# Sorting k and v of two batches in natural layout, on 32x32 tiles of the array

## The chip, the cores and the metric

One core of a Trainium2 chip runs the whole kernel. The metric is device time in microseconds (us) of one execution; lower is better. In this document PE is the matrix engine, ACT and DVE are the scalar and vector engines, POOL is the general-purpose engine (here it issues the loads that cast from 32-bit to bfloat16), and SP is the engine that issues the other transfers. SBUF is the on-chip memory of 128 partitions, PSUM the accumulators that PE writes.

## The reference

Sinkhorn attention feeds a squared-ReLU feed-forward network (FFN). There are 4 batches, 8 heads, 768 tokens, 64 features a head, and 8 blocks of 96 tokens.

```python
P = sort_net                                   # [4, 8, 8, 8]
for _ in range(5):                             # Sinkhorn
    P = exp(P - max(P, -1)); P /= sum(P, -1) + 1e-9; P /= sum(P, -2) + 1e-9
k_sorted = einsum('bhij,bhjcd->bhicd', P, k_blocks)   # blocks of k mixed by P
v_sorted = einsum('bhij,bhjcd->bhicd', P, v_blocks)
attn = softmax(q_block @ k_sorted_block.T / 8)        # within each block
x = (attn @ v_sorted_block), heads side by side       # [3072, 512]
out = relu(x @ w_in) ** 2 @ w_out                     # 512 -> 2048 -> 512
```

## The kernel before

**The FFN** works in eight units of 384 tokens (`ffn_unit`, L662). A unit has 16 upward groups (`up`, L671, matmuls at L675: four of 384 moving columns), each followed by a ReLU on ACT (L683) and a square on DVE (L686), and then 12 downward groups (`down`, L699, matmuls at L703: four of 512 columns; four groups make one output tile of 128 tokens, which is copied out of PSUM at L183 or L185 and stored by SP at L719, over three output buffers). These 28 groups a unit are the planner's clock: its "chunks". A unit reads x transposed (`xT`) for half of one batch.

**Attention** works on pairs of heads, four pairs a batch (class `Unit`, L373). For a pair of batches 2 and 3 the steps are these.

- `s_q` (L386, PE L399): twelve PE transposes of q in two column halves of the array, one for each head, and a copy out of PSUM into `qT`.
- `s_sort` for k (L428, PE L443): twelve matmuls, again in two column halves. The stationary is a 64-feature slice of k as loaded, the moving operand is `w_all`, a 128x128 matrix for each head that holds P spread over the token rows (`build_w`, L358, a product of a mask and P on DVE at L361). The result is k sorted and transposed in one step; a copy brings it into `ksT` with the tokens of a block side by side.
- `s_vn` (L530, PE L542): v is sorted with `w_all` as stationary, one matmul of 384 columns a head, and stays in token rows. To bring the rows of a block onto 96 partitions, SP writes it to DRAM (`v_way`, L563) and reads it back (L568).
- `s_sc` (L467, PE L481): two groups of eight score matmuls (64 feature rows, 96 columns), in two row halves of the array; then the exponential on ACT (L497).
- `s_av` (L580, PE L596): two groups of eight matmuls with the sorted v, and the division by the sums on DVE (L606, L607).
- `s_xt` (L626): the result is turned into `xT` by a transposing transfer on SP (L629).

Batches 0 and 1 sort v in the way of k and turn it back with PE transposes (`s_vt`, L505, PE L513).

**The order of the work** is written by a planner while the program is built (class `Plan`, L50). Each operation is entered with an engine, a cost and what it depends on. PE takes from two queues, attention and FFN, each in its own order; an attention group goes first once its due chunk has come and it is ready, and FFN groups go past an attention group that is not ready. A change of the array's mode is planned at 0.1 us (`SWITCH`). "SP" entries are the issue of a transfer and "WAY" entries its flight. `Ring` objects stand for buffers: among them two PSUM slots for sorts, scores and PV (`r2`). Due chunks are given in `lay` (L798): batch 2 between chunks 84 and 112, batch 3 between 140 and 168, while the FFN units for batches 2 and 3 begin at chunks 112 and 168. So batch 2's attention runs beside the fourth FFN unit and batch 3's beside the sixth; the third and the fifth have none beside them. The loads on POOL are not bound to this order and go out when their buffers are free.

**The start.** Until the first FFN group, the Sinkhorn steps run on ACT and DVE, the loads arrive, and the first half of batch 0's attention runs (list `FIRST`, L19). PE is kept at work by fillers, matmuls on a tile of ones (`fill`, L316): 40 at the beginning (`warm`, L322), and, where the plan has a gap over 0.15 us, one of 128 columns for each 0.08 us of it (L852, L853). A mask for `build_w` is folded out of an identity on POOL (`make_mask`, L268).

Of the kernel before, what the change touches and what calls it, by code (L numbers as in the profile page):

```python
# [8 lines left out]
FP32 = mybir.dt.float32  # L9
# [40 lines left out]
class Plan:  # L50
# [4 lines left out]
    TAIL = {"PE": 0.0, "ACT": 0.09, "DVE": 0.06, "POOL": 0.0, "DMA": 0.0, "SP": 0.0, "WAY": 0.0}  # L55
# [65 lines left out]
def kernel(  # L121
# [47 lines left out]
    rqT, rao, rks, ret = Ring(6), Ring(3), Ring(3), Ring(4)  # L169
    AD = ("ACT", "DVE")  # L170
# [20 lines left out]
    v_r = v.rearrange("b h (p a) d -> b p h (a d)", a=NA)  # L191
    w_in_r = moe_w_in.rearrange("(kc p) f -> p kc f", p=128)
# [29 lines left out]
    v_way = nc.dram_tensor("v_way", (B, 2, 128, NA, HP * 66), BF16, kind="Internal").ap()  # L222
# [9 lines left out]
    w_all = const.tile([128, NH, NB, C0], BF16)  # L232
# [33 lines left out]
    mask = const.tile([128, C0], BF16)  # L266

    def make_mask(e):  # L268

        src, w = ident, 64  # L270
        while w >= C0:
            dst = mask if w == C0 else const.tile([128, w], BF16, name=f"fold{w}")
# [3 lines left out]
    for g in range(HP):  # L276
        load(0, 1, 2 * g, 2)
        load(0, 2, 2 * g, 2)
        if g == 0:
            plan.add("POOL", 1.0, make_mask, [id_op])  # L280
# [35 lines left out]
    def fill(n, w):  # L316
        for _ in range(n):
            nc.tensor.matmul(  # L318
                out=p2[0][:, 1, 512 - w:512], lhsT=ones[:, 0:128], rhs=ones[:, 0:w],
                start=True, stop=True)  # L320

    def warm(e):  # L322
        fill(40, 128)
# [47 lines left out]


    class Unit:  # L373


        def __init__(self, b, hp, halves):
            self.b, self.hp, self.halves = b, hp, halves
            self.n, self.old = rks.take()
# [7 lines left out]
    def s_q(b, hp, p0, p1, due=0, after=None, eng=AD):  # L386
# [4 lines left out]
        def mm(e):  # L391
# [11 lines left out]
            if p0 == 0:  # L403
                tiles["qT", b, hp] = att.tile(
                    [128, NB, NA, C0], BF16, tag="qT", name="qT", bufs=6)

        def ev(e):
            copy(e, tiles["qT", b, hp][:, p0 // C0:p1 // C0, :, :],
# [58 lines left out]
    def s_sc(u, due=0):  # L467
# [3 lines left out]
        for hf in u.halves:  # L471
# [4 lines left out]
            def mm(e, hf=hf, st=st, slot=slot):  # L476
                qT = tiles["qT", u.b, u.hp]
                st["p"] = scp = p2[slot]
                for n in range(NQ):
                    for h in range(2):  # L480
                        nc.tensor.matmul(  # L481
                            out=scp[:, h, BLK * n:BLK * (n + 1)],
                            lhsT=u.ksT[64 * h:64 * (h + 1), hf, BLK * n:BLK * n + 128],
                            rhs=qT[64 * h:64 * (h + 1), NQ * hf + n, :, :]
                            .rearrange("p a c -> p (a c)"),
# [7 lines left out]
            rks.use(u.n, pe)  # L493
# [36 lines left out]
    def s_vn(b, g, due):  # L530

        m, oldm = rvn.take()
        evs = []
        for hp in (2 * g, 2 * g + 1):
            st = {}

            slot, old = r2.take()

            def mm(e, hp=hp, st=st, slot=slot):
                st["p"] = p2[slot]  # L540
                for h in range(2):
                    nc.tensor.matmul(  # L542
                        out=st["p"][:, h, 0:NA * D],
                        lhsT=w_all[:, H * b + 2 * hp + h, :, :].rearrange("p i c -> p (i c)"),
                        rhs=qkv[b][2][:, 2 * hp + h, :],
                        start=True, stop=True)

            def ev(e, hp=hp, st=st):
                h0 = 2 * (hp % 2)
                copy(e, vn_r[m][:, :, h0:h0 + 2, 0:D],  # L550
                     st["p"][:, :, 0:NA * D].rearrange("p e (a d) -> p a e d", d=D))

            s2 = slot
            h0 = H * b + 2 * hp
            pe = plan.add("PE", 0.34, mm, [landed[b, 2, HP * g, 0], built[h0], built[h0 + 1]]
                          + old, due)
            readers[b].append(pe)
            op = plan.add(AD, cost_f(2 * NA * D), ev, [pe] + oldm)
            r2.use(s2, pe, op)
# [326 lines left out]
```

## Time and profile before

| what | us |
|---|---|
| time, median of three runs (lowest to highest) | 235.98 (235.05 to 236.11) |
| the profiled execution: its time | 235.18 |
| its span | 232.8 |
| PE, busy in the span | 225.2 |
| ACT, busy | 125.6 |
| DVE, busy | 107.8 |
| POOL, busy | 27.7 |

The span is the time between the first and the last instruction of the profiled execution. Busy times of different engines overlap. The profile names a group of instructions by its line, its engine, its operation and its operands; a count follows, then the sum of busy time, the mean of one in nanoseconds, and the idle time of the engine before them with what ended it. "PEld" is the loading of stationary operands, which overlaps matmuls. Matmuls are pipelined, so the mean of one is longer than the pace of many. The chain of waits is followed back from the last instruction, and gives each piece's start, its length and what it was.

### The profile page before, as it was taken

The numbers are of one execution on the slowest core, as the hardware profiler recorded it, in microseconds if no ns is written. First come the engines' busy times: TensorE is split into PE (matmuls) and PEld (weight loads), VectorE is DVE, ScalarE is ACT, GpSimd is POOL, SyncE is SP. The second block draws the span as 40 slices with busy tenths as digits, with TensorE's granted clock in tenths as the row PEclk, the third lists the DMA queues.
The fourth block names the chain that finished last, engine by engine and source line by source line (L and its number), as shares of the span: only waits on it lengthen the run. The fifth ranks groups of instructions, "written<-read, shape, count | busy, mean of one in ns | idle before, by whom it ended". The sixth has DMA issues, their size and how long they took to land.

```text
span 232.8 us, 5519 instructions
## 1 busy us (share of the span) xinstructions
PE 225.2 (97%) x2283; PEld 133.3 (57%) x2296; DVE 107.8 (46%) x298; ACT 125.6 (54%) x263; POOL 27.7 (12%) x44
## 2 busy tenths in 40 slices
PE   8997999999999999999999999999999999999994
PEld 8876665556666556445655555445665455446553
DVE  5676677317775515205686425105674225105400
ACT  4665676228884347319865247219776257227521
POOL 8963222400005200000000000000000000000000
PEclk9999999999999999999999999999999999999999
DMA  5999999999914995025511340025612530011012
GB/s 78 202 205 206 206 207 204 203 228 236 156 34 59 176 239 106 3 92 189 139 34 37 83 120 3 0 90 189 139 37 49 85 106 1 31 62 45 0 48 92
DMA packets 33145, 25.70 MB, mean 110 GB/s; under 512 B 9952, under 2 KB 29664, under 8 KB 33120
## 3 DMA queue, kind: packets, MB, share of 16 engines
q0 software_dynamic: 16960, 13.63, 37.8%
q1 hardware_dynamic: 16160, 11.71, 18.3%
q8 instruction: 18, 0.29, 0.5%
q14 instruction: 7, 0.06, 0.1%
HBM read 28.89 MB, written 7.91 MB: 158 GB/s over the span
## 4 chain that ended last, share of the span: by engine, by line
PE 87%; DVE 4%; DMA 3%; ACT 3%; issue 1%; ACTq 0%; DVEq 0%
PE op L703 34%; PE hp L675 32%; PE p L318 4%; PE p L481 3%; PE p L596 3%; PE qtp L399 3%; PE p L443 3%; DMA vblk<-v_way 2%; PE op L737 2%; PE vbp L513 1%; DVE ao L607 1%; ACT h L683 1%; DVE h L686 1%; DMA v_way<-vn 1%; PE xtp L644 1%
## 5 line engine op out<-in xcount | busy, mean ns | idle before, releaser
L675 PE MATMUL hp<-xT,w_in_bf 128*128 128x384 bf16 x512 | 92.3, 326 | 0.0
L703 PE MATMUL op<-w_out_bf,h 128*128 128x512 bf16 x355 | 82.4, 379 | 0.8 <-issue 0.2
L683 ACT ACTIVATE h<-hp 128x384 bf16<-128x384 f32 x128 | 62.7, 494 | 22.0 <-PE hp L675 20.8
L686 DVE TENSOR_TENSOR h<-h 128x384 bf16<-128x384 bf16 x128 | 44.2, 355 | 51.7 <-ACT h L683 51.5
L675 PEld LDWEIGHTS <-w_in_bf 128*128 128x128 bf16 x512 | 46.6, 98 | 29.7
L703 PEld LDWEIGHTS <-h 128*128 128x128 bf16 x368 | 34.7, 98 | 39.0
L183 ACT COPY ob<-op 128x512 f32<-128x512 f32 (+1 forms) x24 | 13.6, 568 | 60.2 <-PE op L703 57.6
L497 ACT ACTIVATE et<-p 96x384 bf16<-96x384 f32 x64 | 26.6, 488 | 9.3 <-PE p L481 9.3
L607 DVE TENSOR_TENSOR ao<-p,rec 96x512 bf16<-96x512 f32 x32 | 22.0, 687 | 1.3 <-DVE rec L606 0.2
L318 PE MATMUL p<-ones 128*128 128x128 bf16 x119 | 11.6, 260 | 1.5 <-DVE ones L200 1.1
L185 DVE CAST vn<-p 128x768 bf16<-128x768 f32 x4 | 3.8, 958 | 19.6 <-PE p L542 19.6
L596 PEld LDWEIGHTS <-et 96*128 96x128 bf16 x256 | 10.8, 97 | 3.4 <-issue 0.5
L183 ACT CAST ksT<-p 128x768 bf16<-128x768 f32 (+1 forms) x13 | 9.5, 730 | 3.4 <-PE p L443 3.3
L606 DVE RECIPROCAL rec<-p 96x8 f32<-96x8 f32 x32 | 6.4, 199 | 10.6 <-PE p L596 9.5
L481 PEld LDWEIGHTS <-ksT 64*128 64x128 bf16 x256 | 6.4, 94 | 7.6 <-issue 4.4
L318 PEld LDWEIGHTS <-ones 128*128 128x128 bf16 x119 | 9.4, 121 | 2.0 <-DVE ones L200 1.1
L481 PE MATMUL p<-qT,ksT 64*128 64x96 bf16 x256 | 10.1, 204 | 0.3 <-DVE ao L607 0.2
L239 POOL DMA_DIRECT2D qb<-in_q_dram x8 | 6.0, 751 | 34.8 <-PE qtp L399 26.4
L185 DVE COPY qT<-qtp 128x768 bf16<-128x768 bf16 x8 | 4.5, 556 | 10.1 <-PE qtp L399 10.1
L399 PEld LDWEIGHTS <-qb 128*64 128x64 bf16 (+1 forms) x240 | 6.4, 109 | 4.7 <-issue 4.0
L185 DVE COPY vs<-vbp 96x512 bf16<-96x512 bf16 (+1 forms) x12 | 6.1, 508 | 6.3 <-PE vbp L513 6.2
L399 PE MATMUL qtp<-ident,qb 128*64 128x128 bf16 (+1 forms) x240 | 8.9, 212 | 0.0
(65 smaller groups left out, 131.8 us busy)
## 6 DMA issues: line engine op xcount, KB each, us to landing
out_dram<-ob SPq DMA_DIRECT2D x23, 256.0 KB, 2.0
qb<-in_q_dram POOLq DMA_DIRECT2D x8, 384.0 KB, 16.0
vb<-in_v_dram POOLq DMA_DIRECT2D x6, 384.0 KB, 17.4
kb<-in_k_dram POOLq DMA_DIRECT2D x6, 384.0 KB, 16.5
w_in_bf<-in_moe_w_in_dram POOLq DMA_DIRECT2D x4, 512.0 KB, 12.6
w_out_bf<-in_moe_w_out_dram POOLq DMA_DIRECT2D x4, 512.0 KB, 17.8
v_way<-vn SPq DMA_DIRECT2D x4, 396.0 KB, 2.4
vblk<-v_way SPq DMA_DIRECT2D x4, 396.0 KB, 4.0
```

The costliest lines, as they stand in the source:

```text
L183: nc.scalar.copy(out=out, in_=in_)
L185: nc.vector.tensor_copy(out=out, in_=in_)
L318: nc.tensor.matmul(out=p2[0][:, 1, 512 - w:512], lhsT=ones[:, 0:128], rhs=ones[:, 0:w], start=True, stop=True)
L399: nc.tensor.transpose(out=t["p"][64 * h:64 * (h + 1), a, :], in_=qb[p0:p1, 2 * hp + h, D * a:D * (a + 1)], identity=ident[p0:p1, p0:p1])
L481: nc.tensor.matmul(out=scp[:, h, BLK * n:BLK * (n + 1)], lhsT=u.ksT[64 * h:64 * (h + 1), hf, BLK * n:BLK * n + 128], rhs=qT[64 * h:64 * (h ...
L497: nc.scalar.activation(out=et[:, h, 0:HS].rearrange("p (n c a) -> p n c a", c=C0, a=NA), in_=st["p"][0:96, h, 0:HS].rearrange("p (n a c) - ...
L596: nc.tensor.matmul(out=oup[:, h, 66 * n:66 * n + D + 1], lhsT=et_r[u.et[hf]][:, h, BLK * n:BLK * n + 128], rhs=(u.vs[:, NQ * hf + n, h, 0: ...
L607: nc.vector.tensor_tensor(out=u.ao[:, n0:n0 + NQ, :, :].rearrange("p n e d -> p e n d"), in0=ov[:, :, :, 0:D], in1=rec[:, :, :, None].to_b ...
L675: nc.tensor.matmul(out=t["hp", nt][:, 0:HS], lhsT=w_in_bf[:, kc, 128 * nt:128 * (nt + 1)], rhs=xT[:, kc, t0:t0 + HS], start=(kc == 0), sto ...
L683: nc.scalar.activation(out=t["h1", nt], in_=t["hp", nt][:, 0:HS], func=AF.Relu)
L686: nc.vector.tensor_tensor(out=t["h2"][:, nt, :], in0=t["h1", nt], in1=t["h1", nt], op=ALU.mult)
L703: nc.tensor.matmul(out=t["op", mt], lhsT=t["h2"][:, nt, 128 * mt:128 * (mt + 1)], rhs=w_out_bf[:, nt, :], start=(nt == 0), stop=(nt == NT ...
```

## The change

Batches 2 and 3 take another way; batches 0 and 1 stay as they are.

- **Loads.** k and v are loaded so that a partition holds 24 tokens of one head in a row, 32 partitions a head, four heads a tile. q is loaded as before.
- **Sort.** `s_nat` replaces `s_vn` for v and `s_sort` for k. With 32 partitions a head the stationary `w_t` has 32 rows and 32 columns: P between blocks, times an identity over the four partitions of a block. Each matmul takes a 32x32 tile of the array: the row group by the head, the column group by the quarter of the 24 tokens; it moves 384 columns. There are eight for a head pair and tensor, planned at 0.2 us in a mode "tile". The result stays in natural layout, and one copy of 128x768 brings it from PSUM to SBUF (as before for k and for v).
- **`w_t`** is built once for both batches by `build_wt`: four short matmuls, two small DVE operations. The mask products for these batches (`build_w`, eight) are gone, and `w_all` is half as large.
- **Transposes.** `s_turn` transposes k by a transposing transfer on SP into `kx`, and q, after a copy on DVE that puts the two heads of a pair side by side, in the same way into `qT`: sixteen more such transfers. The PE transposes of q for these batches are gone.
- **Scores** read their stationary from `kx` with a step of eight elements, and q in runs of 16.
- **v over DRAM** is written by token row and read in runs of 8 x 264 elements instead of 264.
- **Due chunks.** `lay_late` asks for loads at chunk 56 (batch 2) and 112 (batch 3), the sorts 9 and 18 chunks later, the pairs' scores 25, 31, 37 and 43 chunks later, PV and the turn of x three after the scores. The planned flight of a transposing transfer is 1.6 us for 2.2.
- **Fillers.** The first 40 become 10 of 512 columns; gaps over 0.5 us that the plan has before 11 us get wide fillers, one for each 0.33 us.
- **POOL** folds the mask twice more and clears the ends of three `kx` buffers.

```diff
...
-    TAIL = {"PE": 0.0, "ACT": 0.09, "DVE": 0.06, "POOL": 0.0, "DMA": 0.0, "SP": 0.0, "WAY": 0.0}
+    TAIL = {"PE": 0.0, "ACT": 0.09, "DVE": 0.06, "POOL": 0.0, "DMA": 0.0, "SP": 0.0, "WAY": 0.6}
...
+    rkx, rkn, rqi = Ring(3), Ring(3), Ring(2)
...
+    kv_t = [None] + [x.rearrange("b h (c r) d -> b (h c) (r d)", r=4 * NA)
+                     .rearrange("b (g p) x -> b p g x", p=128) for x in (k, v)]
...
-    v_way = nc.dram_tensor("v_way", (B, 2, 128, NA, HP * 66), BF16, kind="Internal").ap()
+    v_way = nc.dram_tensor("v_way", (B, 2, NA, 128, HP * 66), BF16, kind="Internal").ap()
+    kn_r = [const.tile([128, NA, 2, D], BF16, name=f"kn{n}") for n in range(3)]
+    qi_r = [const.tile([128, NA, 2, D], BF16, name=f"qi{n}") for n in range(2)]
+    kx_r = []
+    for n in range(3):
+        kx = const.tile([128, 128 * NB], BF16, name=f"kx{n}")
+        nc.gpsimd.memset(kx[:, 128 * NA:], 0.0)
+        kx_r.append(kx)
...
-    w_all = const.tile([128, NH, NB, C0], BF16)
+    w_all = const.tile([128, NH // 2, NB, C0], BF16)
+    w_t = const.tile([128, NH // 4, 4, NB], BF16)
...
+            if b > 1 and t:
+                return (qkv[b][t].rearrange("p (g h) x -> p g (h x)", h=HP)[:, h0 // HP, :],
+                        kv_t[t][b, :, h0 // HP, :])
...
+        while w >= 4:
+            dst = {C0: mask, 4: mask_t}.get(w) or const.tile([128, w], BF16, name=f"fold{w}")
...
-    def fill(n, w):
-        for _ in range(n):
+    def fill(us, wide=False):
+        if wide:
+            for _ in range(int(us / 0.33)):
+                nc.tensor.matmul(
+                    out=p2[0][:, 0, :].rearrange("p (r x) -> p r x", r=4), lhsT=ones,
+                    rhs=ones[:, None, :].to_broadcast([128, 4, 128]), start=True, stop=True)
+        else:
+            for _ in range(int(us / 0.08)):
+                nc.tensor.matmul(out=p2[0][:, 1, 384:512], lhsT=ones, rhs=ones,
+                                 start=True, stop=True)
...
     def warm(e):
-        fill(40, 128)
+        for _ in range(10):
...
+    def build_wt(due):
...
+        def mm(e):
+            st["p"] = ps1.tile([128, NB, NH // 4], FP32, tag="p1", name="wtp")
+            for h in range(4):
+                nc.tensor.matmul(
+                    out=st["p"][32 * h:32 * (h + 1), :, :].rearrange("p i g -> p (i g)"),
+                    lhsT=pick.rearrange("p j c -> p (j c)"),
+                    rhs=pt.rearrange("p i (g h) -> p h i g", h=4)[:, h, :, :],
+                    start=True, stop=True)
...
+                            lhsT=(u.ksT[64 * h:64 * (h + 1), hf, BLK * n:BLK * n + 128]
+                                  if u.b < 2 else
+                                  kx_r[u.kx][64 * h:64 * (h + 1), NQ * hf + n::NB]),
+                            rhs=(qT[64 * h:64 * (h + 1), NQ * hf + n, :, :]
+                                 .rearrange("p a c -> p (a c)") if u.b < 2 else
+                                 qT[64 * h:64 * (h + 1), :, C0 * (NQ * hf + n):
+                                    C0 * (NQ * hf + n + 1)]),
...
+    def s_nat(b, g, t, due):
...
+                src = qkv[b][t].rearrange("p (g h) x -> p g (h x)", h=HP)
...
+                    r = slice(32 * (2 * (hp % 2) + h), 32 * (2 * (hp % 2) + h + 1))
+                    for c in range(4):
+                        nc.tensor.matmul(
+                            out=p2[slot][32 * c:32 * (c + 1), h, 0:NA * D],
+                            lhsT=w_t[r, HP // 2 * b + g, :, :].rearrange("p c i -> p (c i)"),
+                            rhs=src[r, g, NA * D * c:NA * D * (c + 1)],
+                            start=True, stop=True, tile_position=(r.start, 32 * c))
...
+            pe = plan.add("PE", 0.2, mm, [landed[b, t, HP * g, 0], built["t"]] + old, due,
+                          mode="tile")
...
+            nc.sync.dma_start(out=v_way[b, g].rearrange("a p x -> p a x"),
+                              in_=vn_r[m].rearrange("p a h x -> p a (h x)"))
...
+                out=vb_r[w].rearrange("p i h x -> p (i h x)"),
+                in_=v_way[b, g].rearrange("a (c i) x -> (a c) (i x)", i=NB))
+        wr = plan.add("SP", 0.33, write, evs + [loaded(b)])
+        there = plan.add("WAY", 2.0, lambda e: None, [wr])
+        rd = plan.add("SP", 0.33, read, [there] + oldw)
+        back = plan.add("WAY", 2.0, lambda e: None, [rd])
...
+    def loaded(b):
+        return [landed[b, t, HP, 0] for t in (0,)][0]
+    def s_turn(b, hp):
+        m, op = k_nat[b, hp]
+        kx, oldx = rkx.take()
+        def k_turn(e):
+            nc.sync.dma_start_transpose(
+                out=kx_r[kx][:, 0:128 * NA].rearrange("p (a x) -> p a x", a=NA),
+                in_=kn_r[m].rearrange("p a e d -> p (a e d)"))
+        sp = plan.add("SP", 1.25, k_turn, [op, loaded(b)] + oldx)
+        k_op = plan.add("WAY", 1.6, lambda e: None, [sp])
+        rkn.use(m, k_op)
+        rkx.use(kx, k_op)
+        n, oldi = rqi.take()
+        def q_pair(e):
+            nc.vector.tensor_copy(
+                out=qi_r[n].rearrange("p a e d -> p e a d"),
+                in_=qkv[b][0][:, 2 * hp:2 * hp + 2, :].rearrange("p e (a d) -> p e a d", d=D))
+        qp = plan.add("DVE", 0.5, q_pair, [landed[b, 0, HP * (2 * hp // HP), 0]] + oldi)
+        readers[b].append(qp)
+        rqi.use(n, qp)
+        qTs[b, hp], oldq = rqT.take()
+        def q_turn(e):
+            tiles["qT", b, hp] = att.tile([128, NA, 128], BF16, tag="qT", name="qT", bufs=6)
+            nc.sync.dma_start_transpose(
+                out=tiles["qT", b, hp], in_=qi_r[n].rearrange("p a e d -> p (a e d)"))
+        sp = plan.add("SP", 1.25, q_turn, [qp, loaded(b)] + oldq)
+        q_op = plan.add("WAY", 1.6, lambda e: None, [sp])
+        rqi.use(n, q_op)
+        rqT.use(qTs[b, hp], q_op)
+        return kx, k_op, q_op
...
-            op = plan.add("WAY", 2.2, lambda e: None, [sp])
+            op = plan.add("WAY", 1.6, lambda e: None, [sp])
...
+    def lay_late(b, c0):
+        todo.append((c0, len(todo), lambda due: load_late(b), 0))
+        if b == 2:
+            todo.append((c0, len(todo), build_wt, 0))
+        for g in range(2):
+            for t in (1, 2):
+                todo.append((c0 + 9 + 9 * g, len(todo),
+                             lambda due, g=g, t=t: s_nat(b, g, t, due), b))
+        for hp in range(HP):
+            box = {}
+            def scores(due, hp=hp, box=box):
+                u = box["u"] = Unit(b, hp, (0, 1))
+                u.kx, u.k_op, u.q_op = s_turn(b, hp)
+                s_sc(u, due)
+            c = c0 + 25 + 6 * hp
+            todo.append((c, len(todo), scores, b))
+            todo.append((c + 3, len(todo), lambda due, box=box: s_av(box["u"], due), b))
+            todo.append((c + 3, len(todo), lambda due, box=box: s_xt(box["u"], due), b))
+    def load_late(b):
+        for g in range(2):
+            for t in (1, 2, 0):
+                load(b, t, HP * g, HP)
     lay(0, (1,), 0, n_up)
-    for b, (c0, c1) in enumerate(((n_up, 2 * n_up), (3 * n_up, 4 * n_up), (5 * n_up, 6 * n_up)), 1):
-        lay(b, (0, 1), c0, c1)
+    lay(1, (0, 1), n_up, 2 * n_up)
+    lay_late(2, 2 * n_up)
+    lay_late(3, 4 * n_up)
...
-                fill(int(op.gap / 0.08), 128)
+                fill(op.gap, op.begin < 11 and op.gap > 0.5)
```

More of the change, by code (lines that the diff above doesn't have):

```diff
@@ L266 @@
     mask = const.tile([128, C0], BF16)
+    mask_t = const.tile([128, 4], BF16)
     def make_mask(e):
         src, w = ident, 64
-        while w >= C0:
-            dst = mask if w == C0 else const.tile([128, w], BF16, name=f"fold{w}")
+        while w >= 4:
+            dst = {C0: mask, 4: mask_t}.get(w) or const.tile([128, w], BF16, name=f"fold{w}")
             nc.gpsimd.tensor_tensor(out=dst, in0=src[:, 0:w], in1=src[:, w:2 * w], op=ALU.add)
@@ L279 @@
         if g == 0:
[L280 removed]
+            plan.add("POOL", 1.5, make_mask, [id_op])
     load_w_in(0)
@@ L541, in mm @@
                 for h in range(2):
[L542 to L551, printed above, removed]
```

93 lines of the change are left out of this document (48 added, 45 removed).

## The prediction

> **What bounds the kernel now.** I read the head of the page first, then the busy time by stretch, then the chain of waits in order of time.
>
> ```profile
> span 232.8 us, 5519 instructions
> PE 225.2 (97%) x2283; PEld 133.3 (57%) x2296; DVE 107.8 (46%) x298; ACT 125.6 (54%) x263; POOL 27.7 (12%) x44
> L675 PE MATMUL hp<-xT,w_in_bf 128*128 128x384 bf16 x512 | 92.3, 326 | 0.0
> L703 PE MATMUL op<-w_out_bf,h 128*128 128x512 bf16 x355 | 82.4, 379 | 0.8 <-issue 0.2
> ```
>
> PE is busy 97%, and its two FFN groups hardly wait. The stretches of one FFN unit each (384 tokens) show what attention costs; the columns are length, then busy time by engine.
>
> ```profile
> 84.35:105.11 20.76, 20.71 (x113) 10.96 (x112) 5.74 (x16) 9.62 (x19) 0.00 (x0) 1.00 0.40 90
> 105.11:136.06 30.95, 30.55 (x345) 17.30 (x345) 18.02 (x43) 18.96 (x40) 0.00 (x0) 1.00 0.39 105
> 136.06:156.82 20.76, 20.71 (x113) 10.97 (x113) 5.74 (x16) 9.61 (x19) 0.00 (x0) 1.00 0.10 39
> 156.82:187.97 31.15, 30.80 (x344) 17.21 (x344) 15.99 (x38) 19.75 (x41) 0.00 (x0) 1.00 0.44 104
> 187.97:208.73 20.76, 20.71 (x113) 10.97 (x112) 5.74 (x16) 9.61 (x19) 0.00 (x0) 1.00 0.11 39
> ```
>
> A unit without attention takes 20.76 us. The one with batch 2's attention takes 10.19 us more, the one with batch 3's 10.39. PE idles 0.40 and 0.35 us in these; no other engine passes 20 of 31 us. So what the change takes from or gives to PE there moves the end one for one, wherever the new order puts it. The chain prices the pieces (start, us, what):
>
> ```profile
> 105.11 0.34 PE p L542 x2
> ...
> 107.30 0.46 PE qtp L399 x12
> 107.75 0.76 PE hp L675 x4
> 108.51 0.46 PE p L443 x12
> ...
> 117.07 0.76 PE hp L675 x4
> 117.83 0.46 PE qtp L399 x12
> 118.28 0.34 PE p L443 x12
> 118.62 0.76 PE hp L675 x4
> 119.38 0.25 PE p L596 x8
> 119.63 0.65 PE hp L675 x4
> ...
> 121.18 0.28 PE p L481 x8
> ```
>
> An FFN group of four matmuls takes 0.65 us, so 384 moving columns take 0.163; behind a group that splits the array in column or row halves it takes 0.76. Leaving such a mode costs 0.11. A k sort takes 0.34 behind a q group in the same mode and 0.46 alone: entering costs 0.12.
>
> **What goes.** For the eight head pairs of batches 2 and 3: eight q groups at 0.46 = 3.7 us. Eight k sorts, six at 0.34 and two (the first pair of each batch) at 0.46 = 3.0. Sixteen v matmuls, two in 0.34 = 2.7. Ten exits from the column mode at 0.11 = 1.1. Together **10.5 us** of PE. The check: 20.58 less 10.5 leaves 10.1 for PV (16 groups of 0.25 = 4.0), scores (16 of 0.28 = 4.5, about ten exits = 1.1) and 0.6 of idle, which closes.
>
> **What comes on PE.** 128 matmuls of 384 columns: 8 pairs, k and v, 2 heads, 4 column tiles. They go in eight groups of 16 (two pairs of a tensor; the two PSUM slots make a third pair wait for an eviction, so FFN work stands between groups). Every one of the 16 has its own 32x32 tile. No row shows such tiles. The lower bound goes by the densest issue in the trace, the upper by no overlap at all:
>
> ```profile
> L443 PE MATMUL p<-w_all,kb 128*64 128x128 bf16 x144 | 6.1, 220 | 0.0
> 9.27 0.30 PE qtp L399 x12
> ```
>
> Twelve small transposes in 0.30 are 25 ns each. Sixteen tiles overlapped then take 15 x 0.025 + 0.163 = 0.54, and with both switches (0.23) 0.77 a group: 6.2 us in all. One after another they take 16 x 0.163 + 0.23 = 2.84: 22.7 us. The nearest row is the k sort: 12 matmuls of 128 columns (0.054 each by the FFN rate, 0.65 in a row) take 0.34, so two column halves with different moving data overlap almost fully. I take the overlap to go on to the number of tiles: **6.2 us**, with two at a time (1.30 + 0.23, 12.2 us) as the middle case. Building the small stationary once adds four short matmuls and two switches, about 0.35.
>
> The Trainium skill, "TensorE: Matmul & The Clock Gate", section "The mechanism", speaks against this: a weight load passes a running matmul only where the row group differs, and here four column tiles share each row group. By it the groups go toward the serial end; the k sort above, whose two halves share all rows, disagrees for two tiles.
>
> **Scores** keep count and size, but the stationary k is now read every eighth element, 16 bytes apart, and q in runs of 16 elements. No row shows a strided stationary.
>
> ```profile
> L481 PEld LDWEIGHTS <-ksT 64*128 64x128 bf16 x256 | 6.4, 94 | 7.6 <-issue 4.4
> L481 PE MATMUL p<-qT,ksT 64*128 64x96 bf16 x256 | 10.1, 204 | 0.3 <-DVE ao L607 0.2
> L596 PEld LDWEIGHTS <-et 96*128 96x128 bf16 x256 | 10.8, 97 | 3.4 <-issue 0.5
> ```
>
> A scores group of eight takes 0.28, 35 ns a matmul, close to PV's 31 ns with as many weight columns: loading seems to set the pace in both. Lower bound: no change (the same columns are loaded, which excludes a gain). Upper: every load in the open at its recorded 94 ns, 8 x 0.094 = 0.75, so 16 x 0.47 = +7.5 us. A load at half speed gives 0.56 a group, +4.5. I take **+1.0**, near the contiguous rows, which are all there are.
>
> The Trainium skill, "SBUF — State Buffer", section "Specifications (TRN2)", says that full bandwidth needs two hits per 16-byte line; with one element per line this read would pay on each. By that rule the half-speed sum would hold; no run here shows it yet.
>
> **The start.** Up to the first FFN group PE works through short groups and fillers; the chain (start, us, what), then three rows in order of time (start, us, engine, what):
>
> ```profile
> 7.97 0.78 PE p L318 x12
> ...
> 11.07 0.61 PE p L318 x9
> 11.68 0.13 PE pT L344
> ...
> 24.17 0.76 PE hp L675 x4
> ```
>
> ```profile
> 10.98 0.21 DVE L304 TENSOR_TENSOR pf<-p_sb,cs 32x64 bf16<-32x64 f32 x1
> 4.54 0.33 POOL L273 TENSOR_TENSOR fold<-ident 128x64 bf16<-128x64 bf16 x1
> 6.51 0.23 POOL L273 TENSOR_TENSOR mask<-fold 128x16 bf16<-128x16 bf16 x1
> ```
>
> The Sinkhorn result is ready at 11.19, but its transpose runs only from 11.68, behind nine fillers. A filler planned at 0.08 takes 0.065 (12 in 0.78), so 0.96 of planned gap becomes 0.78. A wide one streams 512 columns, 0.217 by the FFN rate, and is planned at 0.33: the same gap holds two, 0.43. So the transpose can come up to 0.45 earlier (a hop of 0.04 stays). POOL, in front of the loads, gains two folds (0.23 each or a little less) and three memsets of 128x256, which no row shows: 0.1 to 0.4 each by the folds around them, so loads go out 0.7 to 1.6 later. No wait of PE on a load is listed, so that hides behind the fillers; without this cover it costs up to its full 1.6. I take **-0.3**, range -0.4 to +1.2.
>
> **Beside PE.**
>
> ```profile
> L361 DVE TENSOR_TENSOR w_all<-mask,pt 128x256 bf16<-128x256 bf16 x13 | 5.4, 417 | 0.4 <-ACT pt L766 0.4
> L185 DVE COPY qT<-qtp 128x768 bf16<-128x768 bf16 x8 | 4.5, 556 | 10.1 <-PE qtp L399 10.1
> L629 SPq DMA_TRANSPOSE xT<-ao x11: 1213/1218/1318, 58.3 to 184.4; - x11
> DMA to landing us min/median/max: 2.8/2.8/5.5
> 132.52 1.22 SPq L629 DMA_TRANSPOSE xT<-ao  x1
> 135.89 1.30 PE L675 MATMUL hp<-xT,w_in_bf 128*128 128x384 bf16 x7
> ```
>
> DVE loses eight mask products (3.3 us) and gains eight q copies at no more than 0.56 (4.4), while the PSUM copies of q (eight, on ACT or DVE) go and those of k stay as large: nothing, hidden behind PE's stretches, about 1 us if DVE were full. SP gains 16 transposes, 16 x 1.22 = 19.5 us of issue, each landing about 2.8 after its start. What waits behind them on SP are the output stores, and behind these, over three output buffers, the evictions and at last PE's FFN accumulators. Three transposes in a row (3.7 us) stand against three downward groups of 16 x 0.217 = 3.5 each before that bites. K and q turns of a pair are asked for before its scores are due, and the planner lets FFN groups past a head that is not ready, so a late turn moves scores, not PE. The far end is less roomy: batch 2's last transpose is issued at 132.52, lands near 135.3, and the next batch's FFN starts at 135.89; cover 0.6 us, and the same kind of gap stands before batch 3's unit. The loads take longer runs and the v round trip over DRAM has longer reads: both lie off the chain's PE work, nothing either way.
>
> **The sum** against the profiled execution, 235.18 (span 232.8 plus 2.4 around it): -10.5 + 6.2 + 0.35 + 1.0 - 0.3 = -3.25, so 231.9. The median of the three timed runs is 235.98, 0.8 higher; between the two bases I forecast **232.3**.
>
> **Rivals.**
> The strided stationary loads at half speed: +4.5 for +1.0, so **235.8**. For it: scores are paced near their weight loads. Against: the row halves load in turn and may hide it.
>
> Slower than before: the four column tiles of a row group do not run four at a time. Place: the eight sort groups; price: 12.2 at two at a time for 6.2, so **238.3**, and 248.8 one after another. It decides from (10.5 - 0.35 - 1.0 + 0.3) / 8 = 1.18 us a group, or 0.95 without switches, 59 ns a matmul: fewer than 2.8 at a time. For it: the trace shows no more than two tiles at once. Against: these two reach nearly twofold.
>
> Late handover: three transposes a pair on one queue push a batch's last x transpose past the next FFN unit. The cover is 0.6; one turn more ahead (1.22) and a landing delayed as in the slowest row (5.5 for 2.8) cost 1.2 + 2.7 - 0.6 = 3.3 at one of the two handovers, some 1 at the other, so **236.6**. For: there is no FFN work left to fill with. Against: this order finishes scores earlier before the handover.
>
> **Chances.** Forecast 0.60, stride 0.14, two at a time 0.14, handover 0.12. Within 0.5% of 235.98, or 1.2 us, is about what cannot be told from no change. Faster: 0.60 x 0.95 + 0.14 x 0.3 + 0.12 x 0.3 = 0.65; slower: nearly all of two at a time, 0.02 of stride, 0.04 of handover = 0.20; same 0.15. The forecast's own range is 228.9 (the sorts with their switches hidden, 8 x 0.54 = 4.3, no stride cost, 0.4 from the start, on the lower base) to 234.8. To leave out no more than 2 in 10 I reach to two at a time: 228.9 to 238.4.
>
> **What would show it.** Right: the four FFN units from 84.35 on, 103.6 us now, take about 100.7 together, with attention in all four; sort groups of 16 near 0.54 on the chain; scores groups near 0.34. Wrong: a sort group near 1.3 or 2.6, a scores group of 0.5 or more, or PE idle before the first FFN group of a batch with a transpose as releaser. A first FFN group later than 24.1 would speak against the start.

## The result and the profile after

The changed kernel takes **229.86 us** in the median (four executions, 229.81 to 229.89), the kernel before 235.52 beside it (235.05 to 236.11): a ratio of 0.9758, with a 95% interval of 0.9729 to 0.9787. That is 2.4 us under the forecast of 232.3. The profiled execution took 229.89 for 235.18, its span 228.1 for 232.8; the remaining 0.6 us of that difference lies around the span. The profiles of two runs below (q back on PE, four buffers for q) were taken in an execution with a lower granted clock up to 24 and 26 us (0.72 and 0.80), and only what comes behind that is read from them.

The head of the page after:

```profile
span 228.1 us, 5299 instructions
PE 220.0 (96%) x2152; PEld 125.2 (55%) x2165; DVE 106.0 (46%) x295; ACT 122.3 (54%) x260; POOL 27.1 (12%) x49
```

Next the busy time of the kernel after in stretches: from the start of an FFN unit to batch 2's first scores, from there to the end of the next unit, and over the four units in which the work changed; below it that last row of the kernel before. The columns are the stretch, its length, the busy time of PE, PEld, DVE, ACT and POOL, then granted clock, DMA share and GB/s.

```profile
84.02:104.80 20.78, 20.40 (x167) 10.17 (x166) 10.85 (x25) 12.56 (x23) 0.00 (x0) 1.00 0.94 177
104.80:133.62 28.82, 28.70 (x254) 16.47 (x255) 12.13 (x34) 14.76 (x35) 0.00 (x0) 1.00 0.46 112
...
84.02:182.87 98.85, 97.92 (x831) 53.19 (x834) 44.47 (x113) 54.69 (x116) 0.00 (x0) 1.00 0.61 127
```

```profile
84.35:187.97 103.62, 102.76 (x909) 56.43 (x912) 45.48 (x113) 57.95 (x119) 0.00 (x0) 1.00 0.35 89
```

PE still has no idle time to speak of (0.93 us in four units, 0.86 before), so the 4.77 us that these units lost is busy time of PE. Busy time hides short waits: a record of 0.33 us runs on behind the next matmul's start, so that a sort group whose second half waits 0.2 us shows 0.60 us without idle time (at 148.23) where another shows 0.38 (at 146.95). The chain of waits of the kernel after (start, us, what) prices the new pieces:

```profile
23.74 0.76 PE hp L795 x4
...
90.04 0.43 PE p L617 x16
90.47 0.80 ACT kn L184
91.31 0.55 PE p L617 x16
...
94.97 2.85 DMA qT<-qi
98.22 0.96 DVE kn L186
99.23 0.35 PE p L617 x8
...
104.87 0.62 PE p L544 x14
...
147.02 0.31 PE p L617 x16
147.33 0.97 PE op L823 x4
148.30 0.54 PE p L617 x16
...
224.51 0.37 ACT ob L184
```

A sort group of 16 tiles takes 0.31 to 0.55, the scores of a pair of heads (16 matmuls) 0.62. The first FFN group stands at 23.74 for 24.17 before. The last output copy comes 5.10 us earlier (229.61 before); the span shrank by 4.7, so the store behind that copy took 0.4 longer, and why is not shown.

### The profile page after: what moved, and what is told of

It reads as the page before. It is cut to its first block, busy times and chain, and to the rows that moved or that the text cites. A ratio compares the mean times of both kernels' runs of the same rounds, so it can differ in the third digit from the quotient of the medians.

```text
span 228.1 us, 5299 instructions
## 1 busy us (share of the span) xinstructions
PE 220.0 (96%) x2152; PEld 125.2 (55%) x2165; DVE 106.0 (46%) x295; ACT 122.3 (54%) x260; POOL 27.1 (12%) x49
## 4 chain that ended last, share of the span: by engine, by line
PE 81%; ACT 6%; DVE 6%; DMA 4%; issue 2%; POOL 0%; ACTq 0%; DVEq 0%; POOLq 0%
PE op L823 34%; PE hp L795 30%; PE p L544 3%; DVE ao L727 3%; PE p L716 3%; ACT h L803 2%; ACT et L567 2%; DMA qb<-in_q_dram 2%; PE p L503 2%; PE qtp L458 2%; PE op L857 2%; PE vbp L583 1%; PE p L617 1%; DMA qT<-qi 1%; PE p L343 1%
## 5 line engine op out<-in xcount | busy, mean ns | idle before, releaser
L795 PE MATMUL hp<-xT,w_in_bf 128*128 128x384 bf16 x512 | 91.0, 326 | 0.0
L803 ACT ACTIVATE h<-hp 128x384 bf16<-128x384 f32 x128 | 61.5, 497 | 24.1 <-PE hp L795 19.3
L567 ACT ACTIVATE et<-p 96x384 bf16<-96x384 f32 x64 | 26.2, 489 | 5.5 <-PE p L544 5.5
L716 PEld LDWEIGHTS <-et 96*128 96x128 bf16 x256 | 10.7, 97 | 2.9 <-issue 0.3
L253 POOL DMA_DIRECT2D vb<-in_v_dram x10 | 6.6, 659 | 6.4 <-DMA w_in_bf<-in_moe_w_in_dram 3.6
L253 POOL DMA_DIRECT2D kb<-in_k_dram x10 | 6.6, 659 | 6.2 <-DMA w_in_bf<-in_moe_w_in_dram 1.8
L184 ACT CAST ksT<-p 128x768 bf16<-128x768 f32 (+1 forms) x7 | 4.6, 663 | 3.3 <-PE p L503 3.3
L544 PEld LDWEIGHTS <-kx 64*128 64x128 bf16 x128 | 4.6, 155 | 2.8 <-issue 2.8
L716 PE MATMUL p<-vs,et 96*128 96x65 bf16 x128 | 6.0, 193 | 0.0
L716 PE MATMUL p<-vblk,et 96*128 96x65 bf16 x128 | 5.6, 193 | 0.1
L458 PEld LDWEIGHTS <-qb 64*64 64x64 bf16 (+1 forms) x144 | 3.5, 109 | 3.9 <-issue 1.9
L583 PE MATMUL vbp<-ident,vsT 128*128 128x128 bf16 x64 | 5.6, 220 | 0.0
L544 PE MATMUL p<-qT,kx 64*128 64x96 bf16 x128 | 5.6, 226 | 0.0
```

What stands on the lines that cost most here:

```text
L184: nc.scalar.copy(out=out, in_=in_)
L253: nc.gpsimd.dma_start(out=dst, in_=src)
L458: nc.tensor.transpose(out=t["p"][64 * h:64 * (h + 1), a, :], in_=qb[p0:p1, 2 * hp + h, D * a:D * (a + 1)], identity=ident[p0:p1, p0:p1])
L544: nc.tensor.matmul(out=scp[:, h, BLK * n:BLK * (n + 1)], lhsT=(u.ksT[64 * h:64 * (h + 1), hf, BLK * n:BLK * n + 128] if u.b < 2 else kx_r[ ...
L567: nc.scalar.activation(out=et[:, h, 0:HS].rearrange("p (n c a) -> p n c a", c=C0, a=NA), in_=st["p"][0:96, h, 0:HS].rearrange("p (n a c) - ...
L583: nc.tensor.transpose(out=vbp[:, n, :], in_=u.vsT[:, i // NQ, BLK * (i % NQ):BLK * (i % NQ) + 128], identity=ident)
```

## The experiments

All times are medians; each ratio is to the kernel before on the same chip, whose medians lie between 235.26 and 235.83. Differences from the changed kernel's 229.86 are taken between chips, so those of a few tenths of a us are no more than hints.

**The stationary's step.** The scores read k every eighth element. This run reads 128 neighbouring ones; it leaves the right order of the keys out, so its scores are of other keys, in equal number.

```diff
-   kx_r[u.kx][64 * h:64 * (h + 1), NQ * hf + n::NB]),
+   kx_r[u.kx][64 * h:64 * (h + 1), BLK * (NQ * hf + n):BLK * (NQ * hf + n) + 128]),
```

> The scores of batches 2 and 3 read 128 stationary columns that lie side by side in kx instead of every eighth; the tokens are then in the wrong order, so what is left out is the right order of k. Theory (a load with 16-byte steps takes longer and sets the pace of the scores): the stationary load goes from 155 ns back to 94, the two score groups of a pair from 0.62 to about 0.45 on the chain, and the time from 229.86 by 8 x 0.17 = 1.4 to about 228.5. Rival (the loads hide behind the matmuls of the other row half): the load gets shorter but the pair stays at 0.6, and the time within 0.4 of 229.86.

Measured: 228.77 us (228.73 to 229.12), ratio 0.9699 (0.9668 to 0.9731): 1.09 under the changed kernel. The groups by line, first of the kernel after, then of this run (busy us, mean ns, idle before):

```profile
L544 PEld LDWEIGHTS <-kx 64*128 64x128 bf16 x128 | 4.6, 155 | 2.8 <-issue 2.8
L544 PEld LDWEIGHTS <-ksT 64*128 64x128 bf16 x128 | 3.3, 94 | 3.3 <-ACT h L803 1.3 <-issue 0.8 <-ACT ksT L184 0.3
```

```profile
L544 PEld LDWEIGHTS <-kx 64*128 64x128 bf16 x128 | 3.0, 94 | 2.8 <-issue 2.3 <-DMA out_dram<-ob 0.4
```

On the chain a pair takes 0.45 for 0.62 (`104.83 0.45 PE p L544 x16`): 8 x 0.17 = 1.4 us. So much does the step cost on PE; 0.3 of it does not reach the time, because the last pair of each batch then waits for its exponential in PV (`170.86 0.41 PE L716 MATMUL p<-vblk,et 96*128 96x65 bf16 x8 [0.16 <-ACT et L567]`).

**Which steps cost.** The four pairs of a batch read k with steps of 1, 2, 4 and 7 elements of two bytes (other keys again).

```diff
+   kx_r[...][..., NQ * hf + n:NQ * hf + n + 127 * (1, 2, 4, 7)[u.hp] + 1:(1, 2, 4, 7)[u.hp]]),
```

> The scores of batches 2 and 3 read their stationary with steps of 1, 2, 4 and 7 elements for the first, second, third and fourth pair (the tokens are then wrong for all four: what is left out is the right choice of k's columns). Theory (it is lines of 16 bytes that count: full speed needs two elements of a line): 94 ns for steps 1, 2 and 4, near 150 for 7. Rival (any step costs): more than 94 already for 2, rising with the step. Rival (loads read pairs of elements at once): a jump from 1 to 2, and nothing more after.

Measured: 228.85 us in one execution. PE by time in batch 2, one row a pair, in the order of the steps; then a row of the kernel after, with step 8:

```profile
104.78 0.51 PE L544 MATMUL p<-qT,kx 64*128 64x96 bf16 x16
110.38 0.52 PE L544 MATMUL p<-qT,kx 64*128 64x96 bf16 x16
115.33 0.53 PE L544 MATMUL p<-qT,kx 64*128 64x96 bf16 x16
119.83 0.63 PE L544 MATMUL p<-qT,kx 64*128 64x96 bf16 x16
```

```profile
104.80 0.69 PE L544 MATMUL p<-qT,kx 64*128 64x96 bf16 x16
```

The weight loads of the four pairs take 94, 95, 113 and 141 ns in the mean, those with step 8 155. So a step of two elements is free, against both rivals; one of four (8 bytes) lengthens the load by a fifth, against the theory's 94, but a pair hardly shows it; at 7 and 8 a pair costs 0.1 and 0.17 more. The Trainium skill, "SBUF — State Buffer", section "Specifications (TRN2)", asks for two hits per 16-byte line. The pairs agree with it (two at a step of four, about one at 7 and 8); the loads rise by degrees and not at one point. Of a load of 155 ns for 94 the overlap with the matmuls hides a good part.

**The start.** The changed kernel's wide fillers are set back to the narrow ones of before.

```diff
-        if wide:
+        if False:
...
-        for _ in range(10):
-            nc.tensor.matmul(out=p2[0][:, 0, :]..., rhs=ones[:, None, :].to_broadcast([128, 4, 128]), ...)
+        for _ in range(40):
+            nc.tensor.matmul(out=p2[0][:, 1, 384:512], lhsT=ones, rhs=ones, ...)
```

> The changed kernel with the fillers of before (40 of 128 columns, then one of 128 columns for each 0.08 us). Theory A (my step: fillers that overshoot hold up the transpose of the Sinkhorn result): the first FFN group goes from 23.68 back to about 24.1, the time to about 230.3, and the transpose is as late as before. Theory B (what was gained is the 0.64 us pause of PE between two matmuls of one v sort, which stood at 18.54 before and is gone, because fewer PE instructions stand ahead of it): the pause comes back in the same place, the time is about 230.3 too, but the transpose starts at 11.6 in both. Rival (the start did not come from the fillers): the first FFN group stays near 23.7 and the time within 0.2 of 229.86.

Measured: 231.73 us (231.45 to 232.65), ratio 0.9826 (0.9789 to 0.9863): 1.87 more. PE by time around 19 us, of the kernel before and of this run (in brackets the idle time ahead):

```profile
18.19 0.35 PE L443 MATMUL tp<-w_all,vb 128*64 128x64 bf16 x10
19.17 0.22 PE L443 MATMUL tp<-w_all,vb 128*64 128x64 bf16 x2 [0.64 <-issue]
```

```profile
18.48 0.32 PE L502 MATMUL tp<-w_all,vb 128*64 128x64 bf16 x8
19.72 0.25 PE L502 MATMUL tp<-w_all,vb 128*64 128x64 bf16 x4 [0.93 <-issue]
```

PE pauses inside a group, with no wait that the profile shows. Summed over the rows of PE by time, 351 matmuls stand ahead of the pause in both kernels. The first FFN group comes at 24.75, 1.01 later than in the changed kernel. Both theories hold in part: the pause is back with 0.93, and the transpose of the Sinkhorn result stands at 11.78 for 11.56, though the result is no later (11.27 for 11.30). The other 0.86 arises in batch 2, where the shifted order puts a k copy on VectorE behind a q copy that waits for a transpose in flight (3.67 us on the chain).

**Does the pause follow the count?** The same with 34 warm matmuls for 40.

> The narrow fillers of before with six of the forty warm matmuls taken out. Theory (the pause of TensorE near 18.8 us comes at a count of its instructions, 351 matmuls in both kernels that showed it): the pause stands again behind 351 matmuls, so six matmuls further on in the order, and just as long, 0.6 to 0.9 us. Rival (it belongs to a place of the order, a group of v's sort): it stands before the same matmul as with the forty, 345 matmuls from the start.

Measured: 231.88 us in one execution. PE by time:

```profile
18.43 0.38 PE L502 MATMUL tp<-w_all,vb 128*64 128x64 bf16 x12
18.75 0.26 PE L763 MATMUL xtp<-ident,ao 96*128 96x96 bf16 x2
19.43 0.26 PE L763 MATMUL xtp<-ident,ao 96*128 96x96 bf16 x2 [0.43 <-issue]
```

The pause has moved exactly six matmuls on, from behind the eighth of the v group to behind the second of the x transposes: again 351. Its place goes by count, not by work. It is shorter here (0.43), against the expectation's 0.6 to 0.9. But the count alone does not make it: in the changed kernel the 351st matmul is one of the fillers of `22.18 0.61 PE L343 MATMUL p<-ones 128*128 128x128 bf16 x8`, eight in 0.61 us, and no pause stands among them.

**Tiles.** Each of the four column tiles of a head is sorted twice over (the second result overwrites an equal one).

```diff
-                    for c in range(4):
+                    for c in (0, 1, 2, 3, 0, 1, 2, 3):
```

> Every sort group is issued twice, with the same values into the same place: 256 tile matmuls for 128. Theory (the tiles of a group run together, a few ns apart): a second pass waits only for its own tile, so a group of 16 grows from about 0.2 to 0.3 of matmul time by 0.16 to 0.33, and the time by 1.3 to 2.6 us to 231.2 to 232.5. Rival (two at a time): 1.3 us more a group, 10.4 in all, about 240. Rival (one after another): 2.6 a group, about 250.

Measured: 233.1 us (233.06 to 234.98), ratio 0.9911 (0.9872 to 0.995), 3.24 more. On the chain of this run:

```profile
149.75 0.51 PE p L617 x32
...
151.24 0.78 PE p L617 x32
```

Sixteen more tiles cost 0.20 and 0.24 in these two groups (0.31 and 0.54 before), and 0.89 in batch 3 from the start of its unit to its first scores. They run almost at once, and both rivals are out. The time is above the expected range, because batch 2 lost 2.2 in the same stretch: about 0.9 for its groups, and 1.3 that PE waits for a k copy, which on VectorE stands behind a q copy that waits for a transpose.

**The way of q.** Batches 2 and 3 get back q groups on PE in place of copy and DMA transposes; the scores then read q without short runs.

```diff
-                u.kx, u.k_op, u.q_op = s_turn(b, hp)
+                u.kx, u.k_op = s_turn(b, hp)
+                u.q_op = s_q(b, hp, 0, 128, due)
```

> The changed kernel with q of batches 2 and 3 turned by PE as before (twelve transposes and a copy a pair); k and v stay on the tiles. Theory (PE time counts one for one): eight groups at 0.46 and, where FFN work follows, an exit at 0.11, so 3.7 to 4.6 us more: 233.6 to 234.5; the scores groups stay near 0.62 if the stationary's step sets them, and fall if q's short runs do. Rival (the gain came from spreading attention over four FFN units): less than 1.5 us more.

Measured: 233.31 us, ratio 0.9889 (0.9843 to 0.9935), 3.45 more: eight groups of `109.15 0.46 PE qtp L458 x12` are 3.7. A pair's scores stay at 0.63, so the runs of 16 q elements cost nothing, and the whole of it is k's step (reading k in order brought a pair to 0.45 with these runs).

Two buffers for the natural q pairs make VectorE wait for a transpose in flight; this run has four.

```diff
-    rkx, rkn, rqi = Ring(3), Ring(3), Ring(2)
+    rkx, rkn, rqi = Ring(3), Ring(3), Ring(4)
```

> The changed kernel with four buffers for the q pairs instead of two. In the changed kernel's chain of batch 2 a q copy on DVE (at 97.94) waits for the flight of the q transpose two pairs earlier (94.97 to 97.82), the copy of sorted k stands behind it on DVE, and the next sort group on PE behind that. Theory (this wait holds PE for what is left of it, some 0.2 to 0.5 us once, because batch 3 does not show it): 229.4 to 229.7. Rival (PE works on FFN groups meanwhile and loses nothing): within 0.15 of 229.86.

Measured: 229.80 us, ratio 0.9758 (0.9732 to 0.9784): no difference, as the rival said. The wait in the changed kernel (the 2.85 at 94.97 of its chain) is real, but nearly all of it has cover: without it batch 2's first scores come 20.60 behind the start of the unit for 20.79.

**Less cover.** The scores are asked for nine FFN groups later.

```diff
-            c = c0 + 25 + 6 * hp
+            c = c0 + 34 + 6 * hp
```

> Scores, PV and the turn of x are asked for nine chunks later in both batches. In the changed kernel the last x transpose of batch 2 is issued at about 124.5 and lands some 6 us before the next batch's FFN begins at 133.45. Theory (the handover has no price until that cover is used up; nine downward groups last 7.8 us): PE stands for about 2 to 3 us at each of the two handovers, with a transpose as releaser, 233 to 236. Rival (the planner's order hides it, by pulling FFN work of the next unit or by going on earlier than asked): within 1 us of 229.86.

Measured: 240.27 us (239.72 to 241.71), ratio 1.0214 (1.0169 to 1.0258). The waits of this run (in all, times, longest), and its busy time with the granted clock (third column from the right):

```profile
PE hp L795 <- DMA xT<-ao: 6.8, 2, 3.4
```

```profile
137.10:138.50 1.40, 1.40 (x8) 0.82 (x8) 0.36 (x1) 0.84 (x2) 0.00 (x0) 0.87 0.00 0
138.50:141.50 3.00, 3.00 (x12) 1.37 (x10) 1.07 (x3) 1.13 (x3) 0.00 (x0) 0.50 0.00 0
141.50:144.40 2.90, 2.90 (x33) 1.63 (x31) 1.27 (x4) 2.04 (x5) 0.00 (x0) 0.99 0.00 0
```

The late handover exists: PE stands 3.4 us in each batch's first FFN groups (at 133.67, behind three matmuls), with the x transpose as releaser. A us after work goes on, the clock falls to 0.50 for some 3.4 us (0.4 of the first row's 1.40, all of the second, little of the third): 33 matmuls take 7.21 us for 5.37. Waits 6.8 and slow matmuls 2 x 1.84 make 10.5, as measured (10.4). The expected 233 to 236 had the waits, and not the clock behind them. The Trainium skill, "TensorE: Matmul & The Clock Gate", section "What's actually happening", tells of such a window of some 3.4 us; the stand and the slow stretch here are of that size.

**Packing k.** With the right order kept, a copy of the turned k puts the eight orders one behind the other: first on VectorE, then on GpSimd, which also drops three memsets and has three q pair buffers.

```diff
+            nc.vector.tensor_copy(          # second run: nc.gpsimd
+                out=kc_r[kc][:, 0:S].rearrange("p (i r) -> p i r", i=NB),
+                in_=kx_r[kx][:, 0:S].rearrange("p (r i) -> p i r", i=NB))
```

> The changed kernel with one more copy on DVE a pair, which lays the transposed k of each block side by side (768 elements, read every eighth), so that the scores load contiguous columns with the right tokens. Theory (what reading side by side alone gave, 229.86 to 228.77, holds when it is done properly, and DVE has room for eight copies of 0.4 to 0.9 us): 228.7 to 229.0, load 94 ns, pair 0.45. Rival (DVE's order makes something wait behind the new copies, which wait for a flight): 229.5 or more.

> GpSimd, which has no work after the start, copies every turned k into one with the eight orders one behind the other (eight copies of 128x2048; the stationary k of the scores then lies contiguous), and three buffers hold the natural q pairs for two. Theory (the stationary's step costs 0.15 us a group of scores, sixteen groups; the packing lost on VectorE only because it stood in VectorE's order behind the flight of a transpose): weight loads 94 ns, pair of heads 0.45, and no wait of TensorE that names GpSimd: 228.4 to 228.9. Rival (the copy on GpSimd holds VectorE's or the scores' progress, being several us long, or late for the first pair of a batch): 229.6 or more, with a wait on the packed k or longer VectorE copies beside it.

Measured: on VectorE 229.69 us (229.57 to 229.88), ratio 0.9753 (0.9731 to 0.9776), no gain; on GpSimd 228.58 (228.52 to 228.85), ratio 0.971 (0.9683 to 0.9737). A row of each run's waits, for VectorE with the scores' matmuls, whose last column is idle time of PE:

```profile
DVE kc L683 <- DMA kx<-kn: 8.8, 6, 3.5
L549 PE MATMUL p<-qT,kc 64*128 64x96 bf16 x128 | 4.3, 204 | 0.6 <-DVE ao L741 0.5
```

```profile
POOL kc L682 <- DMA kx<-kn: 68.7, 7, 34.0
```

Both wait for the flight of k's transposes, and in both a pair's scores take 0.45. On VectorE the normalizations (`ao`) stand behind that wait, and in batch 2 the scores behind them; on GpSimd nothing does. The GpSimd copy is slower (1574 ns, VectorE's 854), and no wait of PE names it. What the dropped memsets and the third q buffer add to its gain was not run apart.

**The v group.** In the changed kernel a v group takes 0.54 or 0.55 for k's 0.31 to 0.43. With k packed on GpSimd, v's sort now stands eight FFN matmuls behind k's for four.

```diff
-                todo.append((c0 + 9 + 9 * g, len(todo),
+                todo.append((c0 + 9 + 9 * g + 2 * (t - 1), len(todo),
```

> The kernel with k packed on GpSimd, and in it the sort of v stands eight FFN matmuls behind the sort of k for four. Theory (a group of v takes 0.53 to 0.55 for k's 0.31 because its second half waits for the PSUM slot that VectorE still empties of k, 0.96 us an eviction, not because v's tiles run slower): the four groups of v take 0.31 to 0.43 each as k's do, 0.1 to 0.24 less each, together 0.4 to 0.9 us: 227.7 to 228.2. Rival (v's tiles, or their place behind the same kind of group, are slower by themselves): the groups of v stay at 0.53 to 0.55, and the time within 0.3 us of 228.6.

Measured: **226.78 us** (226.63 to 226.84), ratio 0.9632 (0.9607 to 0.9657), the fastest of all: 1.8 under the run before, twice what was expected. PE by time in batch 2, before this step and with it:

```profile
91.03 0.55 PE L621 MATMUL p<-vb,w_t 32*32 32x384 bf16 x16 [0.20 <-ACT kn L184]
...
98.52 0.35 PE L621 MATMUL p<-vb,w_t 32*32 32x384 bf16 x8
99.38 0.35 PE L621 MATMUL p<-vb,w_t 32*32 32x384 bf16 x8 [0.50 <-DVE kn L186]
```

```profile
89.90 0.38 PE L621 MATMUL p<-kb,w_t 32*32 32x384 bf16 x16
90.21 1.47 PE L808 MATMUL hp<-xT,w_in_bf 128*128 128x384 bf16 x8
91.61 0.38 PE L621 MATMUL p<-vb,w_t 32*32 32x384 bf16 x16
```

The v groups had waited for PSUM twice: ahead of them or between their halves (0.20 and 0.50, the releaser is the copy of k), and within a row, where it shows as 0.55 for 0.38. With the waits gone all eight groups take 0.31 on the chain. Over the four units the v groups fell from 2.15 to 1.26 us (from start to next start) and PE's marked idle time from 1.23 to 0.32: the 1.8. From the start of its unit to its first scores batch 3 gained 0.66 (20.50 to 19.84) and batch 2 1.27 (21.22 to 19.95): in batch 2 the copy of k had also stood behind a q copy that waited for a transpose (2.80 us on the chain before this step, none with it), and the expectation had counted the groups alone.

**Batch 1 on the tiles too**, its pairs asked for in the chunks before batch 0's FFN ends, with four q buffers.

```diff
-    lay(1, (0, 1), n_up, 2 * n_up)
+    lay_late(1, n_up - 4)
```

> Batch 1 too is sorted by 32x32 tiles and turned by DMA, with four buffers for the natural q pairs; its pairs are built in the chunks before its end's due time, on FFN work of batch 0. Theory: each of its four pairs gains what a pair of the later batches gained (0.46 q, 0.34 k, 0.34 v, switches, less 0.5 to 0.6 for the tiles and 0.17 for the scores' step, about 1.0 net): some 4 us less, 225.5 to 226.5. Rival: behind the loads of batches 1 and 2, in flight at that time, the turns of batch 1 land late and TensorE stands before its first use of them; then 229 or more, with a wait of over 2 us on a turned k, q or x and perhaps a granted clock below one behind it.

Measured: 246.56 us (245.89 to 247.04), ratio 1.0473 (1.0442 to 1.0505). The waits, and the DMA queue's own rows by time:

```profile
PE p L544 <- DMA qT<-qi: 19.3, 1, 19.3
```

```profile
54.00 8.15 SPq L668 DMA_TRANSPOSE kx<-kn  x1
62.21 8.83 SPq L691 DMA_TRANSPOSE qT<-qi  x1
...
79.60 1.29 SPq L668 DMA_TRANSPOSE kx<-kn  x1
```

While the loads of the next batches are in flight, a transpose takes 8 to 9 us to issue instead of 1.3, and the q transpose begun at 62.21 is the releaser on the chain for 15.63 us. PE stands 19.3 us, and from 70 to 80 us the granted clock is 0.50; the rival held, far beyond its bound of 2 us. That the loads are what holds the transposes is read from the rows (five loads went out between 53 and 57, and the short issues return at 79.6); no run took the loads away.

## Why the prediction was right, point by point

The time lay inside the forecast's own range, 2.4 under the forecast itself; the mechanism was right, and two terms were mis-sized in opposite directions: the sort groups were priced 1.9 too high, and what stands beside PE, put at nothing, let PV take 0.9 more. The four units, forecast at 100.7, took 98.85. Where a term below sums PE's work over the four units, it is the distance from each group's start to the next one's, less marked idle time, in PE's rows by time.

- **PE work removed** (10.5). The k sorts, q groups and v matmuls sum to 3.6, 3.1 and 2.8 there: 9.4, as forecast without the exits (1.1).
- **Sort groups** (6.2, at 0.77 each). They sum to 3.4 in the four units, and with an exit of 0.11 behind each group to 4.3. Some of that is waiting for PSUM inside the v groups. What was mis-sized is the 25 ns between tiles, taken from twelve small transposes. A row of the kernel after: `146.95 0.38 PE L617 MATMUL p<-kb,w_t 32*32 32x384 bf16 x16` holds 16 matmuls of 331 ns (the group's mean), so their starts lie (380 - 331) / 15 = 3.3 ns apart. The Trainium skill, "TensorE: Matmul & The Clock Gate", section "Measured speedup vs the span model", has 4 ns a tile, and the run agrees; the sentence of "The mechanism" that the prediction weighed against it does not hold here, since four successive tiles of a head share their rows and their loads (87 ns each) run while matmuls of the same rows do. Building `w_t` (0.35) stands ahead of the four units; its four matmuls take 0.16 from their start to the next group's. The rival of two tiles at a time needed 1.18 us a group and is out.
- **Scores** (+1.0, bounds 0 to +7.5). Reading k in order gave back 1.09, packing it 1.28 with two other edits: the size was right. That was luck in part, since it was chosen as near the contiguous rows and not worked out; the load does take 1.65 times as long, and half speed as I had priced it, +4.5, assumed that none of it is hidden.
- **Start** (-0.3). The first FFN group came 0.43 earlier, mostly for another reason. The transpose of the Sinkhorn result, which was to gain up to 0.45, stands at 11.56 for 11.61, because the result itself comes 0.32 later (`11.30 0.21 DVE L322 TENSOR_TENSOR pf<-p_sb,cs 32x64 bf16<-32x64 f32 x1` for 10.98), and why is not shown. The fillers themselves did what was forecast: with the narrow ones the changed kernel's transpose stands 0.22 later, at 11.78. The memsets on GpSimd (0.31 each, three of them) moved the first load by 0.24. What brought the gain is that the pause of 0.64 in the kernel before is gone, a row that the prediction did not read.
- **Beside PE** (nothing). True for the q copies, which took 355 ns each and not up to 556. Not foreseen was their wait for the transposes, which landed in 3.9 to 4.2 us in the median and not 2.8; some 0.2 us of batch 2 in the changed kernel, which the time of the run with four buffers does not show, but 0.9 and 1.3 where an experiment shifted the order. Not foreseen either was ACT: the PV groups sum to 4.95 for 4.02 before, most of it in the last pair of each batch (`122.23 0.89 PE L716 MATMUL p<-vblk,et 96*128 96x65 bf16 x16`, 0.66 in the first), whose second half starts when the chain's last exponential ends (at 122.67).
- **Late handover** (0.12). It did not occur: the first FFN matmuls of batches 2's and 3's units follow without a gap. The nine-chunk run shows that its price was rather too low, since the clock falls too (1.84 behind a stand of 3.42).

## What to carry to other kernels

Small matmuls on separate 32x32 tiles cost almost only their first one here (16 in 0.31 us), so once they are there the wait to look at is PSUM's: keep the groups apart by the time of an eviction (0.80 to 0.96 us). A stationary read with a step of up to four bf16 elements cost a pair of scores next to nothing; at eight a copy on an engine with nothing behind it paid, and on one whose other work stood behind it it did not. DMA transposes were a cheap replacement for PE work where no large loads were in flight, and in the one run where they were, a very dear one.

## What was not expected of the hardware

- PE paused for 0.4 to 0.9 us behind its 351st matmul in three kernels, with no releaser, and followed the count when six matmuls were taken out; the changed kernel passes its 351st, at 22.30, without one. The traces leave a rival that no run tests: ahead of each pause a 16 KB packet of the instruction queue (q8 of the page) is in flight, from 16.94, 17.26 and 17.24 and for 0.96 to 0.98 us, and PE goes on 1.2 to 1.5 us after its end. In the changed kernel it runs from 18.72, and the 351st matmul comes 2.6 us after its end. A wait for instructions would look like this.
- Sixteen tile matmuls of 384 columns, 331 ns each by the record, took 0.31 us on the chain.
- A transpose's issue rose from 1.3 to 8.8 us while loads were in flight.
- A stand of PE of 3.4 us was followed by some 3.4 us at a granted clock of 0.50, more than half of the wait's own price again.
